# Lightning attention with an MLP on one core: q and k of tiles from the tenth on transposed by the DMA crossbar, head pairs on the row halves of TensorE

## The chip, the core and the metric

The kernel runs on one core of a Trainium2 chip. Work is done by four compute engines, each with its own in-order instruction stream: TensorE (PE in the profile, with its weight loads listed as PEld), VectorE (DVE), ScalarE (ACT) and GpSimd (POOL). SyncE (SP) only issues transfers. PE writes its results to PSUM, a small accumulation memory; DVE and ACT read PSUM, POOL doesn't. The metric is the device time of one execution in microseconds (us); lower is better.

## The reference

Two layers follow each other. The first is linear attention with a decay `lam` for each head, on q, k, v of shape 4 x 8 x 768 x 64 (batch, heads, positions, head size), in blocks, with a running state `kv_state`:

```python
intra = np.einsum('bhic,bhjc->bhij', qb, kb) * Dmask[None]      # lam**(i-j), i >= j
intra = np.einsum('bhij,bhjd->bhid', intra, vb)
inter = np.einsum('bhid,bhde->bhie', qb * lam_pow[None], kv_state)
out[:, :, sl] = intra + inter
kv_state = lam_block * kv_state + np.einsum('bhsd,bhse->bhde', kb * rev_pow, vb)
```

The second takes x (4 x 768 x 512, the heads side by side), normalises each row and adds an MLP: `x + relu(((x - mu) / std * g_ln) @ w_ch1) @ w_ch2`, with `w_ch1` of 512 x 2048 and `w_ch2` of 2048 x 512.

## The kernel before

**Tiles.** The 3072 rows are cut into NT = 24 tiles of 128 positions, six for each batch element (`nb` = 6), so a state starts anew at tiles 0, 6, 12 and 18. Tiles are counted from 0 here: the tenth is tile 9. NP = 4 is the number of head pairs; a pair fills 128 columns.

**Attention of one tile t.** It is split into steps that are called by name:

- `load_tile` (L56): three transfers of 256 KB for k, q and v, issued on SP; `after_pool` puts a POOL memset ahead so that the load starts no earlier than POOL's stream gets there.
- `p0` (L293): issues the loads of tile t+4 (with two exceptions), then on POOL casts k to bf16 (`kb`) and scales q and v by powers of lam (`qb`, `vb`).
- `p1` (L149): PE transposes `kb` and `qb`, four 128x128 blocks each, into PSUM (`tk`, `tq`). ACT copies `tk` in two halves into `kTp`, a buffer whose other halves stay zero, so that each head of a pair has a 128-row operand of its own. `tq` is copied to `qT`, by ACT in the first four tiles and by DVE later.
- `p2` (L170): the next state (`pk` on PE, sum on DVE, product with `lamC` on POOL into `Sn`), then the scores: eight matmuls `sc` (L192), one for each head, over 128 rows of which 64 are zero, and two DVE products with the mask `tril` into `mA`.
- `p3` (L198): PE forms `po` (eight matmuls with `mA`, four with the state); ACT copies it to `x`; DVE computes mean and variance of `x` (L212, L214) and the centred, scaled `xc` (L216).
- `p4` (L219): `xc` is transposed into the group's `xT`, by PE and ACT for tiles under 8, by a DMA transpose on SP from tile 8 on; then 1/std.

**MLP.** Tiles go through it in groups (`sizes`, L288). `m1` (L250) multiplies 16 blocks of 128 columns of w1 with the group's `xT` (N = 128 times the tiles of the group; groups of one or two tiles take four or two blocks in a unit) and ACT applies relu into `hT`. `m2` (L266) multiplies `hT` with w2, four matmuls of N = 512 in a unit, four units for each tile; the last ends in the DVE operation `o` (L282) and in a store on SP (L284).

**Order.** Every engine executes in the order in which the code issues. The start is written out by hand (L319 to L342), with the weight loads `load_w1` and `load_w2` (1 MB each, read in float32 and written as bf16, issued by POOL). Then come the units of groups 0 to 3 with a table `after` that puts attention steps between them, and from L373 on a planner: `plan` is the list of MLP units of the groups from 4 on, `steps` the list of attention steps in rounds (`round_of`, L306), and after each unit as many steps are issued as `pace` asks for, so that each group's last `p4` is issued some seven units ahead of its first unit. SP's stream is shared by loads, stores and DMA transposes.

Of the kernel before, what the change touches and what calls it, by code (L numbers as in the profile page):

```python
# [7 lines left out]
F32 = mybir.dt.float32  # L8
BF16 = mybir.dt.bfloat16
# [7 lines left out]
def kernel(  # L17
# [38 lines left out]
    def load_tile(t, after_pool=False):  # L56
        b, c = divmod(t, nb)
        got = {}
        for name, src in (("k", k), ("q", q), ("v", v)):
            f = inp.tile([128, H, D], F32, tag=name + "in", name=name + "in")  # L60
            if after_pool:

                nc.gpsimd.memset(f[:, 0, 0:1], 0.0)
                after_pool = False
            nc.sync.dma_start(f, src[b, :, c * C:(c + 1) * C, :].rearrange("h p d -> p h d"))  # L65
            got[name] = f
        qkv_in[t] = got
# [65 lines left out]
    mv_keep = {}  # L133
    xT_of = {}

    def in_k(t, eng):
        kb = wk.tile([128, H, D], BF16, tag="kb", bufs=4, name="kb")
        (eng.copy if eng is nc.scalar else eng.tensor_copy)(kb, qkv_in[t]["k"])  # L138
        st[t] = dict(kb=kb)

    def in_qv(t):
        f = qkv_in.pop(t)
        qb = wk.tile([128, H, D], BF16, tag="qb", name="qb")
        nc.gpsimd.tensor_tensor(qb, f["q"], lam_q[:, :, None].to_broadcast([128, H, D]), op=ALU.mult)  # L144
        vb = wk.tile([128, H, D], BF16, tag="vb", bufs=4, name="vb")
        nc.gpsimd.tensor_tensor(vb, f["v"], lam_v[:, :, None].to_broadcast([128, H, D]), op=ALU.mult)  # L146
        st[t].update(qb=qb, vb=vb)

    def p1(t):  # L149
        s = st[t]  # L150
        tk = ps.tile([128, NP, 128], BF16, tag="aux", bufs=2, name="tk")
        for p in range(NP):
            nc.tensor.transpose(tk[:, p, :], s["kb"][:, 2 * p:2 * p + 2, :], ident)  # L153
        kT = kTp[t % 2]
        nc.scalar.copy(kT[0:64, :, 0, :], tk[0:64, :, :])  # L155
        nc.scalar.copy(kT[64:128, :, 1, :], tk[64:128, :, :])  # L156
        if t < 4:
            tq = ps.tile([128, NP, 128], BF16, tag="mm", bufs=3, name="tq")
        else:
            tq = ps.tile([128, NP, 128], BF16, tag="aux", bufs=2, name="tq")  # L160
        for p in range(NP):
            nc.tensor.transpose(tq[:, p, :], s["qb"][:, 2 * p:2 * p + 2, :], ident)  # L162
        qT = wk.tile([128, NP, 128], BF16, tag="qT", name="qT")
        if t < 4:
            nc.scalar.copy(qT, tq)
        else:
            nc.vector.tensor_copy(qT, tq)  # L167
        s["kT"], s["qT"] = kT, qT

    def p2(t):  # L170
        s = st[t]
        c = t % nb
        s["S"] = state.get("S") if c > 0 else None
        if c < nb - 1:
            pk = ps.tile([128, NP, 128], F32, tag="aux", bufs=2, name="pk")
            for p in range(NP):
                nc.tensor.matmul(pk[:, p, :], lhsT=s["kb"][:, 2 * p:2 * p + 2, :], rhs=s["vb"][:, 2 * p:2 * p + 2, :],  # L177
                                 start=(p == 0), stop=(p == NP - 1), skip_group_check=True)
            Sn = wk.tile([128, NP, 128], BF16, tag="S", name="Sn")
            if c == 0:  # L180
                nc.vector.tensor_tensor(Sn, pk, lamC, op=ALU.mult)
            else:
                tmp = wk.tile([128, NP, 128], F32, tag="Stmp", bufs=2, name="Stmp")
                nc.vector.tensor_tensor(tmp, pk, state["S"], op=ALU.add)  # L184
                nc.gpsimd.tensor_tensor(Sn, tmp, lamC, op=ALU.mult)  # L185
            state["S"] = Sn
        mA = wk.tile([128, H, 128], BF16, tag="mA", name="mA")
        for half in range(2):
            sc = ps.tile([128, H // 2, 128], F32, tag="sc", bufs=2, name="sc")
            for i in range(H // 2):  # L190
                h = half * (H // 2) + i
                nc.tensor.matmul(sc[:, i, :], lhsT=s["kT"][:, h // 2, h % 2, :], rhs=s["qT"][:, h // 2, :],  # L192
                                 start=(i == 0), stop=(i == H // 2 - 1), skip_group_check=True)
            nc.vector.tensor_tensor(mA[:, half * (H // 2):(half + 1) * (H // 2), :], sc,  # L194
                                    tril[:, None, :].to_broadcast([128, H // 2, 128]), op=ALU.mult)
        s["mA"] = mA

    def p3(t):  # L198
        s = st[t]
        po = ps.tile([128, H, D], F32, tag="po", bufs=1, name="po")  # L200
        inter = s["S"] is not None
        for h in range(H):
            nc.tensor.matmul(po[:, h, :], lhsT=s["mA"][:, h, :], rhs=s["vb"][:, h, :],  # L203
                             start=(h == 0), stop=(not inter and h == H - 1), skip_group_check=True)
        if inter:
            for p in range(NP):
# [9 lines left out]
        nc.vector.scalar_tensor_tensor(xc, in0=x, scalar=mv[:, 0:1], in1=g_row, op0=ALU.subtract, op1=ALU.mult)  # L216
        s["xc"], s["mv"], s["x"] = xc, mv, x

    def p4(t):  # L219
# [65 lines left out]

        return m1, m2

    sizes = [2, 2, 1, 1, 2, 2, 3, 4, 4, 3]  # L288
    groups = [list(range(sum(sizes[:i]), sum(sizes[:i + 1]))) for i in range(len(sizes))]
    assert groups[-1][-1] == NT - 1  # L290
    group_of = {t: g for g, ts in enumerate(groups) for t in ts}

    def p0(t):  # L293
        for n in {4: (), 5: (8, 9)}.get(t, (t + 4,)):
            if n < NT:
                load_tile(n)
        in_k(t, nc.gpsimd)
        in_qv(t)


    def p3_p0(t):
# [2 lines left out]
            p0(t + 3)  # L304

    def round_of(j):  # L306
        steps = [(p1, j), (p3_p0, j - 1), (p2, j)]
        if j <= 11:
            steps.append((p4, j - 1))
        elif j > 12:  # L310
            steps.append((p4, j - 2))
        return [(f, t) for f, t in steps if t < NT]

    def run(*steps):
        for f, *a in steps:
            f(*a)


    for t in range(2):  # L319
        in_k(t, nc.vector)  # L320
        in_qv(t)
# [9 lines left out]
    in_qv(3)  # L331
    load_w1(1)
    load_tile(4, after_pool=True)
    run((p2, 2), (p4, 0), (p1, 3), (p3, 2))
    load_w1(2)
    load_w1(3)
    run((p2, 3), (p4, 1), (p0, 4))
    for c in range(NWC):
        load_w2(c)
    load_tile(5, after_pool=True)  # L340
# [30 lines left out]


    steps = []  # L373
    for j in range(8, NT + 2):
        steps += [s for s in round_of(j) if s not in ((p3_p0, 7), (p4, 7))]

    def upto(g):
# [48 lines left out]
```

## Time and profile before

| | us |
|---|---|
| median of 3 runs (236.11 to 236.44) | 236.11 |
| the profiled execution | 235.61 |
| its span, first to last instruction | 233.9 |
| PE busy (1792 matmuls) | 212.4 |
| ACT / DVE / POOL busy | 114.3 / 113.3 / 90.1 |

The profile has rows for each group of instructions by source line (L...), the chain of work that ended last, and, for chosen stretches, the busy time of each engine. A `pm` is a product of `m1` (L258) or `m2` (L271); `kin`, `qin`, `vin` are the loaded inputs, `w` a weight. The operations of before that the change touches on ACT and DVE:

```profile
L155 ACT COPY kTp<-tk 64x512 bf16<-64x512 bf16 x24 | 13.7, 572 | 31.4 <-PE tk L153 31.4
...
L216 DVE SCALAR_TENSOR_TENSOR xc<-x,mv,g_row 128x512 bf16<-128x512 f32 x24 | 20.7, 862 | 0.9
...
L167 DVE COPY qT<-tq 128x512 bf16<-128x512 bf16 x20 | 8.4, 419 | 15.2 <-PE tq L162 15.1
...
L156 ACT COPY kTp<-tk 64x512 bf16<-64x512 bf16 x24 | 13.9, 581 | 0.6
```

Read: line, engine, operation, output and input, shape and type, count; then busy us and mean ns of one; then the engine's idle time just before them and what ended it.

### The profile page before, as it was taken

The page shows a single profiled execution, that of the slowest core. Times are in us where ns is not written, and L with a number is a line of the kernel's source. Part 1 is how long each engine was busy: PE and PEld are TensorE (multiplying, and loading weights), DVE is VectorE, ACT ScalarE, POOL GpSimd, SP SyncE. Part 2 cuts the span into 40 slices and gives each one's busy share as a digit, 9 for nine tenths or more (in the row PEclk, how much of TensorE's full clock was granted, in tenths as well). Part 3 has the DMA queues.
Part 4 walks back from the last instruction along what each step waited for, and adds up shares of the span by engine and source line. Part 5 has one row for each costly group of instructions (what it writes and reads, how often), then busy time and mean ns, then how long its engine had stood idle before and what let it go on. Part 6 is the DMA issues. An engine that isn't in the chain of part 4 may idle for free.

```text
span 233.9 us, 4503 instructions
## 1 busy us (share of the span) xinstructions
PE 212.4 (91%) x1792; PEld 136.8 (58%) x1792; DVE 113.3 (48%) x219; ACT 114.3 (49%) x222; POOL 90.1 (39%) x103
## 2 busy tenths in 40 slices
PE   0664899999999899989999999999999999999992
PEld 0453879644977596579567655555554544456540
DVE  3459530334665567868776656653573223220021
ACT  5765486421546465367437832678213664017400
POOL 2659526216834667952746940633220000000000
PEclk9997799999999999999999999999999999999998
DMA  6998996999999999999999903310011200411012
GB/s 125 221 225 113 221 176 89 182 217 205 225 209 300 204 242 227 209 210 243 168 249 229 160 3 112 93 22 3 34 66 59 67 0 3 125 60 39 3 66 70
DMA packets 91717, 32.02 MB, mean 137 GB/s; under 512 B 84272, under 2 KB 88624, under 8 KB 91696
## 3 DMA queue, kind: packets, MB, share of 16 engines
q1 hardware_dynamic: 87328, 27.53, 58.7%
q0 software_dynamic: 4224, 4.19, 11.3%
q8 instruction: 14, 0.23, 0.4%
q14 instruction: 7, 0.06, 0.1%
q10 hardware_dynamic: 144, 0.00, 0.0%
HBM read 27.53 MB, written 6.29 MB: 145 GB/s over the span
## 4 chain that ended last, share of the span: by engine, by line
PE 70%; DMA 15%; SPq 4%; POOL 4%; DVE 3%; ACT 2%; issue 1%; DVEq 0%; ACTq 0%
PE pm L271 30%; PE pm L258 28%; DMA vin<-in_v_dram 7%; DMA w<-in_moe_w_ch_dram 6%; SPq L65 4%; PE sc L192 3%; PE po L203 2%; DMA xT<-xc 2%; PE tq L162 2%; PE po L207 1%; PE tk L153 1%; POOL vb L146 1%; PE pk L177 1%; DVE xc L216 1%; POOL w L78 1%
## 5 line engine op out<-in xcount | busy, mean ns | idle before, releaser
L258 PE MATMUL pm<-xT,w 128*128 128x256 bf16 (+3 forms) x640 | 90.4, 294 | 1.5 <-DMA xT<-xc 0.8
L271 PE MATMUL pm<-w,hT 128*128 128x512 bf16 x384 | 88.6, 379 | 0.1
L261 ACT ACTIVATE hT<-pm 128x512 bf16<-128x512 f32 (+1 forms) x104 | 58.2, 565 | 44.5 <-PE pm L258 43.6
L258 PEld LDWEIGHTS <-w 128*128 128x128 bf16 x640 | 56.2, 98 | 25.4 <-DMA xT<-xc 1.0
L271 PEld LDWEIGHTS <-hT 128*128 128x128 bf16 x384 | 36.3, 98 | 38.0 <-issue 0.4
L185 POOL TENSOR_TENSOR Sn<-Stmp,lamC 128x512 bf16<-128x512 f32 x16 | 20.4, 1273 | 60.9 <-DVE Stmp L184 60.9
L212 DVE BATCH_NORM_STATS2 stats<-x 128x6 f32<-128x512 f32 x24 | 16.7, 694 | 43.6 <-ACT x L210 43.5
L282 DVE SCALAR_TENSOR_TENSOR o<-pm,rstd,x 128x512 f32<-128x512 f32 (+1 forms) x25 | 18.0, 725 | 33.6 <-PE pm L271 33.3
L194 DVE TENSOR_TENSOR mA<-sc,tril 128x512 bf16<-128x512 f32 x48 | 30.7, 681 | 1.3 <-PE sc L192 1.3
L144 POOL TENSOR_TENSOR qb<-qin,lam_q 128x512 bf16<-128x512 f32 x24 | 25.6, 1066 | 13.7 <-DMA qin<-in_q_dram 13.6
L155 ACT COPY kTp<-tk 64x512 bf16<-64x512 bf16 x24 | 13.7, 572 | 31.4 <-PE tk L153 31.4
L146 POOL TENSOR_TENSOR vb<-vin,lam_v 128x512 bf16<-128x512 f32 x24 | 25.5, 1062 | 3.9 <-DMA vin<-in_v_dram 2.8
L210 ACT COPY x<-po 128x512 f32<-128x512 f32 x24 | 14.0, 585 | 16.0 <-PE po L207 12.5
L216 DVE SCALAR_TENSOR_TENSOR xc<-x,mv,g_row 128x512 bf16<-128x512 f32 x24 | 20.7, 862 | 0.9
L192 PE MATMUL sc<-qT,kTp 128*128 128x128 bf16 x192 | 16.4, 234 | 0.3 <-ACT kTp L156 0.2
L167 DVE COPY qT<-tq 128x512 bf16<-128x512 bf16 x20 | 8.4, 419 | 15.2 <-PE tq L162 15.1
L153 PE MATMUL tk<-ident,kb 128*128 128x128 bf16 x96 | 10.0, 231 | 6.1 <-DVE kb L138 5.5
L138 POOL CAST kb<-kin 128x512 bf16<-128x512 f32 x20 | 13.2, 661 | 5.7 <-DMA kin<-in_k_dram 5.5
L192 PEld LDWEIGHTS <-kTp 128*128 128x128 bf16 x192 | 13.5, 106 | 1.6 <-ACT kTp L156 0.4
L156 ACT COPY kTp<-tk 64x512 bf16<-64x512 bf16 x24 | 13.9, 581 | 0.6
L162 PE MATMUL tq<-ident,qb 128*128 128x128 bf16 x96 | 9.7, 227 | 3.9 <-POOL qb L144 3.5
L203 PEld LDWEIGHTS <-mA 128*128 128x128 bf16 x192 | 9.0, 99 | 6.7 <-DVE mA L194 3.4
(45 smaller groups left out, 112.5 us busy)
## 6 DMA issues: line engine op xcount, KB each, us to landing
kin<-in_k_dram SPq DMA_DIRECT2D x24, 256.0 KB, 4.9
qin<-in_q_dram SPq DMA_DIRECT2D x24, 256.0 KB, 5.0
vin<-in_v_dram SPq DMA_DIRECT2D x24, 256.0 KB, 5.4
out_dram<-o SPq DMA_DIRECT2D x23, 256.0 KB, 2.5
w<-in_moe_w_ch_dram POOLq DMA_DIRECT2D x8, 512.0 KB, 8.0
g_row<-in_moe_g_ln_dram SPq DMA_DIRECT2D x1, 256.0 KB, 5.0
xT<-xc SPq DMA_TRANSPOSE x16, 3.2
out_dram<-o SPq DMA_DIRECT2D x2, 128.0 KB, 1.7
```

The source lines that it names most:

```text
L144: nc.gpsimd.tensor_tensor(qb, f["q"], lam_q[:, :, None].to_broadcast([128, H, D]), op=ALU.mult)
L146: nc.gpsimd.tensor_tensor(vb, f["v"], lam_v[:, :, None].to_broadcast([128, H, D]), op=ALU.mult)
L162: nc.tensor.transpose(tq[:, p, :], s["qb"][:, 2 * p:2 * p + 2, :], ident)
L185: nc.gpsimd.tensor_tensor(Sn, tmp, lamC, op=ALU.mult)
L192: nc.tensor.matmul(sc[:, i, :], lhsT=s["kT"][:, h // 2, h % 2, :], rhs=s["qT"][:, h // 2, :], start=(i == 0), stop=(i == H // 2 - 1), skip ...
L194: nc.vector.tensor_tensor(mA[:, half * (H // 2):(half + 1) * (H // 2), :], sc, tril[:, None, :].to_broadcast([128, H // 2, 128]), op=ALU.mult)
L212: nc.vector.bn_stats(stats, x)
L216: nc.vector.scalar_tensor_tensor(xc, in0=x, scalar=mv[:, 0:1], in1=g_row, op0=ALU.subtract, op1=ALU.mult)
L258: nc.tensor.matmul(pm[:, b, :], lhsT=w1[n // W2K][:, kk, (n % W2K) * 128:(n % W2K + 1) * 128], rhs=xT_of[g][:, kk, 0:N], start=(b == 0 and ...
L261: nc.scalar.activation(hT[:, u * NB:(u + 1) * NB, 0:N], pm, ACT.Relu)
L271: nc.tensor.matmul(acc[i], lhsT=hT[:, kk, i * 128:(i + 1) * 128], rhs=w2[kk // W2K][:, kk % W2K, :], start=(kk == 0), stop=(kk == KB - 1))
L282: nc.vector.scalar_tensor_tensor(o[:, sl], in0=a[:, sl], scalar=rstd, in1=x[:, sl], op0=ALU.mult, op1=ALU.add)
```

## The change

1. From tile 9 on (`XB = 9`), `kb` and `qb` are the two halves of one tile `kq` (128 x 1024 bf16), and `p1` is one DMA transpose on SP of `kq` into `kqT`, in place of eight PE transposes and the copies. It stands one round earlier than `p1` did.
2. In all tiles the scores take the two heads of a pair from partitions 0 to 63 and 64 to 127 of `kT` and `qT`, with 64-row operands, and write to two PSUM tiles, one for each half; the zero-padded `kTp` and its memsets go, and in tiles 0 to 8 ACT copies `tk` once.
3. `xc` is computed from `po` in PSUM and no longer from `x`.
4. `p0` loads tile t+2 and no longer t+4. The groups are 2, 2, 1, 1, 2, 2, 2, 3, 3, 3, 3 tiles, so `m1` runs at N up to 384. `p4` of tile j-1 is in round j throughout.
5. At the start the scores stand ahead of the state; `load_w1(0)` is issued before `vb` of tile 2, the POOL product of a state after the inputs of the next tile, and the first `p4` steps are in other places.

The diff, cut to its core:

```diff
-    kTp = []
-    for i in range(2):
-        kt = const.tile([128, NP, 2, 128], BF16, name=f"kTp{i}")
-        nc.vector.memset(kt, 0.0)
-        kTp.append(kt)
+    XB = 9
+
     def in_k(t, eng):
-        kb = wk.tile([128, H, D], BF16, tag="kb", bufs=4, name="kb")
+        if t >= XB:
+            kq = wk.tile([128, 2, H, D], BF16, tag="kq", bufs=4, name="kq")
+            kb, qb = kq[:, 0], kq[:, 1]
...
     def p1(t):
         s = st[t]
+        if t >= XB:
+            kqT = wk.tile([128, 2 * NP, 128], BF16, tag="kqT", name="kqT")
+            nc.sync.dma_start_transpose(kqT, s["kq"].rearrange("p a h d -> p (a h d)"))
+            s["kT"], s["qT"] = kqT[:, 0:NP, :], kqT[:, NP:2 * NP, :]
+            return
...
-        kT = kTp[t % 2]
-        nc.scalar.copy(kT[0:64, :, 0, :], tk[0:64, :, :])
-        nc.scalar.copy(kT[64:128, :, 1, :], tk[64:128, :, :])
+        kT = wk.tile([128, NP, 128], BF16, tag="kT", name="kT")
+        nc.scalar.copy(kT, tk)
...
+    def scores(t):
+        s = st[t]
+        mA = wk.tile([128, 2, NP, 128], BF16, tag="mA", name="mA")
+        sc = [ps.tile([128, NP, 128], F32, tag="sc", bufs=2, name=f"sc{e}") for e in range(2)]
+        for p in range(NP):
+            for e in range(2):
+                half = slice(e * D, (e + 1) * D)
+                nc.tensor.matmul(sc[e][:, p, :], lhsT=s["kT"][half, p, :], rhs=s["qT"][half, p, :],
+                                 start=(p == 0), stop=(p == NP - 1), skip_group_check=True)
+        for e in range(2):
+            nc.vector.tensor_tensor(mA[:, e], sc[e], tril[:, None, :].to_broadcast([128, NP, 128]), op=ALU.mult)
...
-                nc.gpsimd.tensor_tensor(Sn, tmp, lamC, op=ALU.mult)
+                s["pool"] = lambda: nc.gpsimd.tensor_tensor(Sn, tmp, lamC, op=ALU.mult)
...
-        nc.vector.scalar_tensor_tensor(xc, in0=x, scalar=mv[:, 0:1], in1=g_row, op0=ALU.subtract, op1=ALU.mult)
+        nc.vector.scalar_tensor_tensor(xc, in0=po.rearrange("p h d -> p (h d)"), scalar=mv[:, 0:1], in1=g_row, op0=ALU.subtract, op1=ALU.mult)
...
-    sizes = [2, 2, 1, 1, 2, 2, 3, 4, 4, 3]
+    sizes = [2, 2, 1, 1, 2, 2, 2, 3, 3, 3, 3]
...
     def p0(t):
-        for n in {4: (), 5: (8, 9)}.get(t, (t + 4,)):
-            if n < NT:
-                load_tile(n)
+        if 5 < t < NT - 2:
+            load_tile(t + 2)
...
     def round_of(j):
-        steps = [(p1, j), (p3_p0, j - 1), (p2, j)]
-        if j <= 11:
-            steps.append((p4, j - 1))
-        elif j > 12:
-            steps.append((p4, j - 2))
+        steps = [(p1, j)] if j < XB else []
+        if j + 1 >= XB:
+            steps.append((p1, j + 1))
+        steps += [(p3_p0, j - 1), (p2, j)]
+        steps.append((p4, j - 1))
...
-    run((p1, 0), (p2, 0), (p1, 1), (p3, 0))
+    run((p1, 0), (scores, 0), (next_state, 0), (p1, 1), (scores, 1), (p3, 0), (next_state, 1))
     in_k(2, nc.scalar)
-    in_qv(2)
+    in_q(2)
     load_w1(0)
-    run((p2, 1), (p1, 2), (p3, 1))
+    in_v(2)
+    fin_state(1)
+    run((p1, 2), (scores, 2), (p3, 1), (next_state, 2))
...
-    run((p2, 2), (p4, 0), (p1, 3), (p3, 2))
+    run((p4, 0), (p1, 3), (scores, 3), (p4, 1), (p3, 2))
```

Three places show how the order moves. The first is PE's stream at tile 9, from the end of its state product `pk` into its scores; before, where `kTp_131` is the padded buffer of odd tiles:

```order
L177 LDWEIGHTS kb
L177 MATMUL pk<-vb,kb 128x128
L192 LDWEIGHTS kTp_131
L192 MATMUL sc<-qT,kTp_131 128x128
L192 LDWEIGHTS kTp_131
L192 MATMUL sc<-qT,kTp_131 128x128
```

and now, where `sc_1360` and `sc_1361` are the PSUM tiles of the even and the odd heads:

```order
L198 LDWEIGHTS kq
L198 MATMUL pk<-vb,kq 128x128
L185 LDWEIGHTS kqT
L185 MATMUL sc_1360<-kqT 128x128
L185 LDWEIGHTS kqT
L185 MATMUL sc_1361<-kqT 128x128
```

The count of score matmuls is the same, eight; they alternate between two outputs and take weights and moving operand from `kqT`, which a DMA writes. The eight transposes `tk` and `tq` of the tile (L153, L162) are gone from PE's stream.

The second place is SP's stream at the first DMA transposes of `xc`, those of tiles 8 and 9; before, with the loads of tile 16 between them and those of tile 17 behind:

```order
L227 DMA_TRANSPOSE xT<-xc 128x4x128
L65 DMA kin<-in_k_dram 128x8x64
L65 DMA qin<-in_q_dram 128x8x64
L65 DMA vin<-in_v_dram 128x8x64
L227 DMA_TRANSPOSE xT<-xc 128x4x128
L284 DMA out_dram<-o 128x512
```

and now, with `kqT` of tile 11 and the loads of tile 14 between the two, and `kqT` of tile 12 behind:

```order
L248 DMA_TRANSPOSE xT<-xc 128x4x128
L156 DMA_TRANSPOSE kqT<-kq 128x8x128
L65 DMA kin<-in_k_dram 128x8x64
L65 DMA qin<-in_q_dram 128x8x64
L65 DMA vin<-in_v_dram 128x8x64
L248 DMA_TRANSPOSE xT<-xc 128x4x128
L305 DMA out_dram<-o 128x512
L156 DMA_TRANSPOSE kqT<-kq 128x8x128
```

One DMA transpose of twice the size has come into each round, and the loads beside it are of a tile nearer at hand.

The third place is POOL's stream at the start, from the inputs of tile 2 to the last load of w1; before:

```order
L144 TENSOR_TENSOR qb<-qin,lam_q 128x512
L146 TENSOR_TENSOR vb<-vin,lam_v 128x512
L75 DMA w_0_75<-in_moe_w_ch_dram 128x4x512
L185 TENSOR_TENSOR Sn<-Stmp,lamC 128x512
L144 TENSOR_TENSOR qb<-qin,lam_q 128x512
L146 TENSOR_TENSOR vb<-vin,lam_v 128x512
L75 DMA w_1_76<-in_moe_w_ch_dram 128x4x512
L63 MEMSET kin 128x1
L185 TENSOR_TENSOR Sn<-Stmp,lamC 128x512
L75 DMA w_2_77<-in_moe_w_ch_dram 128x4x512
L75 DMA w_3_78<-in_moe_w_ch_dram 128x4x512
```

and now:

```order
L145 TENSOR_TENSOR qb<-qin,lam_q 128x512
L75 DMA w_0_75<-in_moe_w_ch_dram 128x4x512
L149 TENSOR_TENSOR vb<-vin,lam_v 128x512
L206 TENSOR_TENSOR Sn<-Stmp,lamC 128x512
L145 TENSOR_TENSOR qb<-qin,lam_q 128x512
L149 TENSOR_TENSOR vb<-vin,lam_v 128x512
L75 DMA w_1_76<-in_moe_w_ch_dram 128x4x512
L206 TENSOR_TENSOR Sn<-Stmp,lamC 128x512
L63 MEMSET kin 128x1
L75 DMA w_2_77<-in_moe_w_ch_dram 128x4x512
L75 DMA w_3_78<-in_moe_w_ch_dram 128x4x512
```

The first weight load has passed `vb` of tile 2, and the memset that lets the loads of tile 4 go on SP has fallen behind the state product of tile 2.

More of the change, by code (lines that the diff above doesn't have):

```diff
@@ L168, in p1, with next_state @@
         s["kT"], s["qT"] = kT, qT
-    def p2(t):
+    def scores(t):
[9 more added lines that the diff above has]
+            nc.vector.tensor_tensor(mA[:, e], sc[e], tril[:, None, :].to_broadcast([128, NP, 128]), op=ALU.mult)
+        s["mA"] = mA
+    def next_state(t):
         s = st[t]
@@ L184, in p2, with fin_state @@
                 nc.vector.tensor_tensor(tmp, pk, state["S"], op=ALU.add)
-                nc.gpsimd.tensor_tensor(Sn, tmp, lamC, op=ALU.mult)
+                s["pool"] = lambda: nc.gpsimd.tensor_tensor(Sn, tmp, lamC, op=ALU.mult)
             state["S"] = Sn
[L187 to L196, printed above, removed]
+    def fin_state(t):
+        f = st[t].pop("pool", None)
+        if f:
+            f()
+    def p2(t):
+        next_state(t)
+        fin_state(t)
+        scores(t)
     def p3(t):
@@ L202, in p3 @@
         for h in range(H):
-            nc.tensor.matmul(po[:, h, :], lhsT=s["mA"][:, h, :], rhs=s["vb"][:, h, :],
+            nc.tensor.matmul(po[:, h, :], lhsT=s["mA"][:, h % 2, h // 2, :], rhs=s["vb"][:, h, :],
                              start=(h == 0), stop=(not inter and h == H - 1), skip_group_check=True)
@@ L293, in p0 @@
     def p0(t):
-        for n in {4: (), 5: (8, 9)}.get(t, (t + 4,)):
-            if n < NT:
-                load_tile(n)
+        if 5 < t < NT - 2:
+            load_tile(t + 2)
         in_k(t, nc.gpsimd)
-        in_qv(t)
+        in_q(t)
+        in_v(t)
     def p3_p0(t):
@@ L320 @@
         in_k(t, nc.vector)
-        in_qv(t)
+        in_q(t)
+        in_v(t)
     lam_cp = lam_c.rearrange("p (a two) -> p a two", two=2)
@@ L373 @@
     steps = []
-    for j in range(8, NT + 2):
+    for j in range(8, NT + 1):
         steps += [s for s in round_of(j) if s not in ((p3_p0, 7), (p4, 7))]
```

23 lines of the change are left out of this document (14 added, 9 removed).

## The prediction

> **What bounds the kernel now.** I read the chain that ended last first, in order of time (start, us, what).
>
> ```profile
> 23.55 11.34 DMA vin<-in_v_dram
> 34.96 1.04 POOL vb L146
> 36.01 2.22 POOL w L78 x3
> 38.22 13.75 DMA w<-in_moe_w_ch_dram
> 52.02 4.48 PE pm L271 x20
> 56.49 0.22 PE tk L153 x4
> 56.72 0.22 PE tq L162 x4
> 56.94 1.73 PE pm L271 x8
> 58.66 0.45 PE sc L192 x8
> ```
>
> Up to 52.02 the chain is made of transfers: v of tile 4, the POOL product that waits for it, and behind that product in POOL's stream the issue of w2, whose last quarter lands at 51.97. From there on it is PE. The busy time of PE in stretches (stretch, length, PE busy, matmuls, clock, DMA share, GB/s) says how full PE is:
>
> ```profile
> 52.02:229.56 177.54, 174.71 (x1452) 1.00 0.63 128
> 66.00:106.00 40.00, 37.20 (x429) 1.00 1.12 231
> 106.00:229.56 123.56, 123.52 (x882) 1.00 0.41 84
> ```
>
> All of PE's 2.83 us of idle time after 52 lies between 66 and 106. PE's timeline has it in five places (start, length, instruction, [idle before, releaser]):
>
> ```profile
> 70.88 0.38 PE L234 MATMUL xt<-ident,xc 128*128 128x128 bf16 x4 [0.47 <-DVE qT L167]
> 77.61 0.40 PE L234 MATMUL xt<-ident,xc 128*128 128x128 bf16 x4 [0.85 <-DVE xc L216]
> 81.57 0.56 PE L192 MATMUL sc<-qT,kTp 128*128 128x128 bf16 x7 [0.22 <-ACT kTp L156]
> 100.12 1.05 PE L258 MATMUL pm<-xT,w 128*128 128x256 bf16 x8 [0.85 <-DMA xT<-xc]
> 104.67 0.38 PE L162 MATMUL tq<-ident,qb 128*128 128x128 bf16 x4 [0.40 <-DVE Sn L181]
> ```
>
> So there are two stages: until 52 the time is that of DMA, and work taken from PE there is worth nothing; after 52 each us taken from PE's stream is a us of the result, as long as no new wait opens.
>
> **The change part by part**, against the profiled execution (235.61, span 233.9; the median of the runs is 0.5 above it).
>
> *Transposes of tiles 9 to 23.* Four `tk` and four `tq` cost PE 0.22 + 0.22 in the chain above, at every tile. Fifteen tiles: 15 x 0.44 = **6.6 us less**, all after 52. The trace shows these transposes back to back at 55 ns each. The Trainium skill (TensorE: Matmul & The Clock Gate, Part 4) gives some 275 ns for a transpose in a kernel's context; by it the 120 would be worth 33 us, an estimate from that page; the row of this trace decides.
>
> *Scores on row halves.* Tiles 5 to 23 run their scores after 52: 19 times 0.45, 56 ns a matmul. If the two halves run side by side, eight matmuls take the time of four, 0.22, and 19 x 0.23 = 4.4 us go. Against that stands what PE loses when it changes between full and half operands, twice for each tile. No row of before has half operands. The nearest rows bound it: differently shaped neighbours (transposes, N = 64, N = 512) follow each other without a gap, so nothing; or the whole length of one score matmul less its step.
>
> ```profile
> L192 PE MATMUL sc<-qT,kTp x192: 219/219/314, 9.2 to 187.4; 128*128 128x128 bf16 x192
> ```
>
> That is 219 - 56 = 163 ns a change, 0.33 a tile. The tile then takes 0.22 to 0.55 in place of 0.45: from -4.4 to +1.9 us over 19 tiles. I take half the price, since neither end has a row of its own kind: 0.39, **1.1 us less**. If the halves don't overlap at all, the price stands without the gain: +6.3.
>
> The Trainium skill has both sides (TensorEngine Tiling (Array Packing), Theoretical Speedup and Key Properties): two row tiles give up to twice the speed, and a change of the tiling mode drains TensorE. No run here shows either yet; the page gives no length of a drain.
>
> *MLP groups.* The steps of `m1` by N are in the chain:
>
> ```profile
> 105.05 0.87 PE pm L258 x8
> ...
> 122.77 1.30 PE pm L258 x8
> ...
> 150.88 1.73 PE pm L258 x8
> ```
>
> That is 0.109 at N = 256, 0.163 at 384, 0.216 at 512. Before: 256, 128 and 128 of them, 76.4 us; now 320 and 256, none at 512, 76.6; the 128 of single-tile groups stay. Some **0.1 us more**.
>
> *The start.* The single copy of `tk`, the missing memsets and the earlier scores shorten the way to the first `m1`, at 26.50 before, though `xc` of tile 1 was ready at 21.5 (one row each from the timelines of DVE, POOL and PE):
>
> ```profile
> 18.90 2.63 DVE L216 SCALAR_TENSOR_TENSOR xc<-x,mv,g_row 128x512 bf16<-128x512 f32 x1
> 22.22 1.26 POOL L185 TENSOR_TENSOR Sn<-Stmp,lamC 128x512 bf16<-128x512 f32 x1 [0.39 <-DVE Stmp L184]
> 26.50 2.10 PE L258 MATMUL pm<-xT,w 128*128 128x256 bf16 x16 [0.67 <-ACT xT L235]
> ```
>
> The transposes (0.40) and their copy (0.59) must still come between, so up to 3 to 4 us could be won there. It is covered: w2 lands at 51.97 whatever PE does, because its issue waits for v of tile 4. On POOL that load's memset has fallen behind a 1.26 us product, so the three loads leave SP up to 1.3 later. But w1 keeps the DMA engines at work meanwhile and the bytes are the same. **Nothing**, bounds -0.4 (w1's last quarters leave earlier by the 0.39 wait) to +1.3. If the cover goes, the start is worth -3.
>
> *Copies and centring.* ACT loses 48 half copies for 9 whole ones, DVE 15 copies `qT`. Both engines are half idle and no chain after 52 but two of the waits runs through them. `xc`, 862 ns on average in the row shown with the profile of before, is with a PSUM input like `o`, the same kind of operation:
>
> ```profile
> L282 DVE SCALAR_TENSOR_TENSOR o<-pm,rstd,x 128x512 f32<-128x512 f32 (+1 forms) x25 | 18.0, 725 | 33.6 <-PE pm L271 33.3
> ```
>
> No slower, so nothing; `po` is held some 2 us longer, and the next `p3` is a round away.
>
> *Waits.* The 0.22 goes (the second copy of `tk`), the 0.40 too (no `tq` left that needs a PSUM buffer): **0.6 us less**. The 0.47 and 0.85 at `xt` stay, since tiles 6 and 7 still go po, copy, mean, `xc`, transpose, with one or two units between. What is new is that PE's score weights of tile 9 on wait for a DMA, with PE's whole stream behind them. And SP, in order, holds loads, `kqT`, `xT` and stores: a `kqT` that waits for POOL's `qb` holds back the next loads, and an `xT` waits behind them. SP's price of each (start, us):
>
> ```profile
> 62.61 1.13 SPq L65 DMA_DIRECT2D qin<-in_q_dram  x1
> ...
> 93.86 0.52 SPq L65 DMA_DIRECT2D kin<-in_k_dram  x1
> 94.48 0.53 SPq L65 DMA_DIRECT2D qin<-in_q_dram  x1
> 95.10 0.87 SPq L65 DMA_DIRECT2D vin<-in_v_dram  x1
> 96.06 1.55 SPq L227 DMA_TRANSPOSE xT<-xc  x1
> 97.71 0.53 SPq L284 DMA_DIRECT2D out_dram<-o  x1
> ```
>
> and of all DMA transposes (min/median/max, ns on SP, then us from issue to landing):
>
> ```profile
> L227 SPq DMA_TRANSPOSE xT<-xc x16: 1191/1518/1924, 92.3 to 203.1; - x16
> ...
> DMA to landing us min/median/max: 2.4/3.2/5.9
> ```
>
> `kqT` is two of these: 2.4 to 3.8 on SP, some 3 in the middle, and a landing 1 to 2 later than that of an `xT`, 4 to 8. A round then costs SP 1.9 for loads, 1.5, 3.0 and 0.5, together **7.0**. A round of PE, from the first transposes of tile 8 to the last `po`:
>
> ```profile
> 79.59 0.39 PE L153 MATMUL tk<-ident,kb 128*128 128x128 bf16 x4
> 195.19 0.40 PE L203 MATMUL po<-vb,mA 128*128 128x64 bf16 x8
> ```
>
> is 115.6 / 16 = 7.2, less about 0.5 now, 6.7. SP is just at PE's pace, and falls behind by 0.3 a round over the 13 rounds that still load, 4 us. `kqT` is issued about one and a half rounds ahead of its scores, 10 us, and outlasts that. `xT` has about six us from its issue to the group's first unit, so one or two group starts may wait as the one at 100.12 does, by 0.85. I leave that one as it is, and put the new waits at 0, bounds 0 and +4.
>
> Sum: 235.6 - 6.6 - 1.1 + 0.1 + 0 - 0.6 = 227.4 for a profiled execution, **227.9** for the median.
>
> **The rivals.**
>
> - *The halves run for nothing.* No cost of a change, as for all other changes of shape in the trace: 3.3 us more go, 224.6. For it: eight `po` weight loads pass in 0.23 us, so weights can follow at the 28 ns that this needs. Against: no row with half operands.
> - *The price of a change is the full 0.163.* Two a tile cost more than the overlap gives: 3.0 more than the forecast, 230.9. It is the drain rule named above, with a length from the row of L192.
> - *The halves don't do what is said*: the two matmuls of a pair run one after the other and pay the changes too, 227.9 + 6.3 + 1.1 = 235.3, no measurable or a small gain.
> - *The start counts after all*: w2 lands earlier with PE, 3 us less, 224.9. Against: its issue stands behind the load of tile 4 in both orders.
> - *SP becomes the bound, slower than before.* If loads cost 1.13 each, as at 62.61, SP's round is 3.4 + 1.55 + 3.1 + 0.5 = 8.6. Over 13 rounds its lag grows by 1.9 each, 25 us, of which 10 are the lead of `kqT`: 15 us of waits, 227.9 + 15 = 243. It decides from a round of SP above 6.7 + 10/13 = 7.5, and makes the kernel slower than before from 8.1. For it: loads cost that much wherever DMA was full. Against: they did so when loads ran four tiles ahead; now they go at PE's pace, and at 93 to 98 with transposes between them they took 0.5 to 0.9.
>
> **How the numbers follow.** Forecast 0.38, free halves 0.27, full price of the change 0.18, halves without effect 0.05, the start 0.05, SP as the bound 0.07. The likeliest gives 227.9. The range takes in free halves with some more waits gone (223.5) and the full price with a us of new waits (232): it leaves out the halves without effect and SP as the bound, 0.12, and some tails. A measurement here can tell about 0.2% (0.5 us) from no change. Faster: all but two cases, 0.88. Slower: SP, 0.07. Same: the rest, 0.05.
>
> **What would show it.** Before 52, the last w2 still lands near 52 and PE waits for it longer than the 0.25 or so of before. After 52, PE's stream has no `tk` and `tq` from tile 9 on, and the chain has eight score matmuls in 0.39; 0.22 or 0.55 and more tell the rivals. PE's idle time between 66 and 106 is about 2.2. SP's DMA transposes of `kqT` take 2.4 to 3.8 and land before their scores; a wait `sc <- DMA kqT`, tile after tile, shows the slow case. I'm wrong if PE is idle after 106, or if w2 lands more than a us away from 52.

## The result and the profile after

The changed kernel took **227.72 us** (median of 4 runs, 227.62 to 228.95) against 236.11 (236.04 to 236.44) before: a ratio of **0.965**, 95% interval 0.962 to 0.969. Its profiled execution took 227.68, with a span of 226.0. One execution of e2 below (232.26) fell into a slower state of the core and is left out of its median and range.

The stretches of PE that were shown of before (stretch, length, PE busy, matmuls, clock, DMA share, GB/s) now read:

```profile
53.05:221.85 168.80, 167.65 (x1397) 1.00 0.77 157
66.00:106.00 40.00, 38.89 (x424) 1.00 1.16 218
106.00:221.85 115.85, 115.81 (x838) 1.00 0.60 128
```

53.05 is the begin of the fourth round of `m2`, the first work that needs the last quarter of w2; it stood at 52.02. From there PE needs 168.8 where it needed 177.5. PE's timeline has the waits that matter:

```profile
29.29 0.40 PE L255 MATMUL xt<-ident,xc 128*128 128x128 bf16 x4 [0.54 <-DVE xc L237]
31.27 10.57 PE L279 MATMUL pm<-xT,w 128*128 128x256 bf16 x80 [1.59 <-DMA w<-in_moe_w_ch_dram]
...
71.66 0.40 PE L255 MATMUL xt<-ident,xc 128*128 128x128 bf16 x4 [0.24 <-DVE xc L237]
78.30 0.40 PE L255 MATMUL xt<-ident,xc 128*128 128x128 bf16 x4 [0.75 <-DVE xc L237]
```

After 53, two of before's five waits are left. Ahead of it stands something new: the 80 matmuls at 31.27 take 10.57 us (before, the same 80 took 8.90), since the granted clock was 0.64 from 31.27 to 36.00. The chain shows a tile's steps (start, us, what):

```profile
130.51 0.65 PE pm L279 x4
131.16 0.22 PE pk L198 x4
131.38 0.33 PE sc L185 x8
131.72 4.66 PE pm L279 x28
```

No `tk`, no `tq`; the eight scores take 0.33 in place of 0.45 (the experiments show that another 0.10 stands ahead of them). The view of the source line of the new DMA transposes:

```profile
L156 SPq DMA_TRANSPOSE kqT<-kq x15: 1242/1283/2167, 81.5 to 175.6; - x15
...
DMA to landing us min/median/max: 3.0/3.2/4.6
```

In the median they cost SP 1.28 and land in 3.2, about what an `xT` of half the size takes (1.23 and 3.5 here).

### The profile page after: what moved, and what is told of

Read it like the earlier page. It is cut to its first block, busy times and chain, and to the rows that moved or that the text cites. A ratio compares the mean times of both kernels' runs of the same rounds, so it can differ in the third digit from the quotient of the medians.

```text
span 226.0 us, 4339 instructions
## 1 busy us (share of the span) xinstructions
PE 206.9 (92%) x1736; PEld 131.4 (58%) x1736; DVE 104.5 (46%) x202; ACT 95.5 (42%) x191; POOL 88.0 (39%) x103
## 4 chain that ended last, share of the span: by engine, by line
PE 81%; DMA 6%; DVE 4%; SPq 3%; ACT 2%; issue 1%; POOL 1%; DVEq 0%
PE pm L292 36%; PE pm L279 35%; DMA w<-in_moe_w_ch_dram 4%; PE sc L185 3%; SPq L65 3%; DMA qin<-in_q_dram 2%; PE po L224 2%; PE po L228 2%; PE pk L198 1%; DVE stats L233 1%; ACT x L231 1%; DVE xc L237 1%; PE tq L169 1%; DVE Stmp L205 1%; PE xt L255 1%
## 5 line engine op out<-in xcount | busy, mean ns | idle before, releaser
L279 PE MATMUL pm<-xT,w 128*128 128x256 bf16 (+2 forms) x704 | 92.2, 287 | 1.6 <-DMA w<-in_moe_w_ch_dram 1.6
L282 ACT ACTIVATE hT<-pm 128x384 bf16<-128x384 f32 (+1 forms) x112 | 60.0, 536 | 57.9 <-PE pm L279 57.2
L279 PEld LDWEIGHTS <-w 128*128 128x128 bf16 x704 | 63.6, 100 | 23.9 <-DMA w<-in_moe_w_ch_dram 1.8
L292 PEld LDWEIGHTS <-hT 128*128 128x128 bf16 x384 | 36.2, 98 | 39.2
L237 DVE SCALAR_TENSOR_TENSOR xc<-po,mv,g_row 128x512 bf16<-128x512 f32 x24 | 18.0, 751 | 2.3
L145 POOL TENSOR_TENSOR kq<-qin,lam_q 128x512 bf16<-128x512 f32 x15 | 15.7, 1044 | 1.2 <-DMA qin<-in_q_dram 1.2
L145 POOL TENSOR_TENSOR qb<-qin,lam_q 128x512 bf16<-128x512 f32 x9 | 9.4, 1042 | 15.3 <-DMA qin<-in_q_dram 14.7
L205 DVE TENSOR_TENSOR Stmp<-pk,Sn 128x512 f32<-128x512 f32 x16 | 10.9, 683 | 4.2 <-PE pk L198 4.1
L224 PE MATMUL po<-vb,mA 128*128 128x64 bf16 x192 | 10.4, 199 | 0.1
L141 POOL CAST kq<-kin 128x512 bf16<-128x512 f32 x15 | 9.2, 611 | 2.0 <-DMA kin<-in_k_dram 2.0
L258 ACT ACTIVATE std<-mv,eps_t 128x1 f32<-128x1 f32 x24 | 7.0, 293 | 5.4 <-DVE mv L235 5.4
```

The costliest lines, as they stand in the source:

```text
L145: nc.gpsimd.tensor_tensor(st[t]["qb"], qkv_in[t]["q"], lam_q[:, :, None].to_broadcast([128, H, D]), op=ALU.mult)
L224: nc.tensor.matmul(po[:, h, :], lhsT=s["mA"][:, h % 2, h // 2, :], rhs=s["vb"][:, h, :], start=(h == 0), stop=(not inter and h == H - 1), ...
L237: nc.vector.scalar_tensor_tensor(xc, in0=po.rearrange("p h d -> p (h d)"), scalar=mv[:, 0:1], in1=g_row, op0=ALU.subtract, op1=ALU.mult)
L279: nc.tensor.matmul(pm[:, b, :], lhsT=w1[n // W2K][:, kk, (n % W2K) * 128:(n % W2K + 1) * 128], rhs=xT_of[g][:, kk, 0:N], start=(b == 0 and ...
L282: nc.scalar.activation(hT[:, u * NB:(u + 1) * NB, 0:N], pm, ACT.Relu)
L292: nc.tensor.matmul(acc[i], lhsT=hT[:, kk, i * 128:(i + 1) * 128], rhs=w2[kk // W2K][:, kk % W2K, :], start=(kk == 0), stop=(kk == KB - 1))
```

## The experiments

All are edits of the changed kernel. They ran on other chips, on which the kernel before took 236.5 to 237.1 with a wider spread, so each has its ratio to the runs beside it. The last four columns are of the profiled execution: where the fourth round of `m2` begins; from there to PE's last matmul; PE's waits of 0.15 and more in that stretch; and the difference of the two, PE's **work**.

| kernel | median us (range) | ratio, 95% | round 4 | to the end | waits | work |
|---|---|---|---|---|---|---|
| before | 236.11 | 1 | 52.02 | 177.50 | 2.79 | 174.71 |
| after | 227.72 (227.62-228.95) | 0.962-0.969 | 53.05 | 168.76 | 0.99 | 167.77 |
| e2 halves apart | 228.68 (228.27-229.44) | 0.959-0.971 | 52.55 | 171.04 | 2.89 | 168.15 |
| e3 `pk` between | 230.40 (230.09-230.68) | 0.967-0.977 | 52.74 | 171.94 | 1.00 | 170.94 |
| f1 one half | 232.01 (231.17-233.78) | 0.972-0.986 | 55.22 | 172.71 | 1.00 | 171.71 |
| e4 PE transposes | 235.09 (233.76-236.62) | 0.989-0.998 | 53.83 | 175.11 | 1.00 | 174.11 |
| f2 full rows | 234.49 (234.02-235.14) | 0.983-0.995 | 51.84 | 176.13 | 1.44 | 174.69 |
| g2 loads far | 237.93 (235.40-238.93) | 1.002-1.009 | 52.78 | 179.08 | 8.72 | 170.36 |
| g3 centre x | 228.49 (228.09-228.94) | 0.963-0.968 | 53.03 | 170.15 | 2.40 | 167.75 |
| e1 load 4 first | 228.29 (227.73-228.62) | 0.958-0.968 | 52.86 | 169.91 | 1.83 | 168.08 |
| f3 w2 early | 229.88 (227.95-230.35) | 0.961-0.974 | 52.68 | 171.43 | 3.74 | 167.69 |
| f4 w1, w2 early | 228.00 (227.77-228.13) | 0.955-0.967 | 51.52 | 170.74 | 3.04 | 167.70 |
| g1 tile 4 early | 227.37 (226.67-228.41) | 0.958-0.967 | 51.64 | 169.20 | 1.25 | 167.95 |
| h1 start | 227.28 (226.66-227.88) | 0.958-0.964 | 51.90 | 170.06 | 2.37 | 167.69 |

Work repeats within 0.4 us between kernels that issue the same PE instructions at the full clock (g2's fell, see there), so it separates what PE does from what it waits for.

### What the scores on row halves are worth

**e2** takes the halves one after the other.

```diff
-        for p in range(NP):
-            for e in range(2):
+        for e in range(2):
+            for p in range(NP):
```

> The eight score matmuls of a tile issued as four of the even heads and then four of the odd ones, nothing else changed. In the changed kernel a tile's scores take 0.42 us from the end of the matmul ahead to the start of the one behind, against 0.45 before. Theory A, the halves of a pair overlap (0.22) and the rest is two changes of the operand height at 0.10 each: apart, the matmuls take 0.45 + 0.20 = 0.65 a tile, and 19 tiles make the kernel 4.4 us longer, 232.1. Theory B, the halves don't overlap, and a 64-row matmul is simply shorter: no change, 227.7 within 0.3.

**e3** puts `pk` between the second and the third pair (`scores(t, next_state)` for `next_state(t)` and `scores(t)`; the diff is cut to its core).

```diff
+            if p == 1 and between:
+                between(t)
```

> The state product pk of a tile (four full-height matmuls) is put between the second and third pair of its scores, so each tile with a state product has four changes of operand height and not two; the matmuls are the same. Theory A, a change costs 0.10 us: 15 tiles after 53 us with two more changes, 3.0 us longer, 230.7. Theory B, a change costs nothing and the 0.42 of the scores is incomplete overlap: within 0.3 of 227.7.

**f1** uses one half alone: it leaves out the odd heads' scores and computes those of the even heads twice.

```diff
-                half = slice(e * D, (e + 1) * D)
+                half = slice(0, D)
```

> The odd heads' scores are left out: the even heads' operands are used twice, so that all eight score matmuls of a tile lie on the same row half. Theory A (the two halves of a pair run side by side on PE, each half no faster than a full matmul): with one half there is nothing beside it, eight score matmuls take 0.44 in place of 0.22, +0.22 a tile, x19 = +4.2 us: about 232. Theory B (a matmul of 64 rows by itself comes every 28 ns, whichever half it is on): nothing changes, 227.7, and the eight still take 0.22.

The rows of one tile in PE's timelines, first of the changed kernel, then of e2, e3 and f1. Read the starts; the lengths count each matmul's way through the array, so that neighbours overlap:

```profile
130.35 0.81 PE L279 MATMUL pm<-xT,w 128*128 128x384 bf16 x4
131.00 0.39 PE L198 MATMUL pk<-vb,kq 128*128 128x128 bf16 x4
131.32 0.40 PE L185 MATMUL sc<-kqT 64*128 64x128 bf16 x8
131.65 4.72 PE L279 MATMUL pm<-xT,w 128*128 128x384 bf16 x28
```

```profile
132.69 0.39 PE L198 MATMUL pk<-vb,kq 128*128 128x128 bf16 x4
133.01 0.41 PE L185 MATMUL sc<-kqT 64*128 64x128 bf16 x8
133.35 3.91 PE L279 MATMUL pm<-xT,w 128*128 128x384 bf16 x23
```

```profile
131.95 0.81 PE L280 MATMUL pm<-xT,w 128*128 128x384 bf16 x4
132.70 0.29 PE L185 MATMUL sc<-kqT 64*128 64x128 bf16 x4
132.91 0.40 PE L200 MATMUL pk<-vb,kq 128*128 128x128 bf16 x4
133.24 0.29 PE L185 MATMUL sc<-kqT 64*128 64x128 bf16 x4
133.46 3.75 PE L280 MATMUL pm<-xT,w 128*128 128x384 bf16 x22
```

```profile
135.36 0.39 PE L198 MATMUL pk<-vb,kq 128*128 128x128 bf16 x4
135.68 0.62 PE L185 MATMUL sc<-kqT 64*128 64x128 bf16 x8
136.23 0.99 PE L279 MATMUL pm<-xT,w 128*128 128x384 bf16 x5
```

In the changed kernel the four `pm` (0.163 each) end their steps at 131.00 and `pk` follows without a gap. Four `pk` are 0.22, so 0.10 lies between `pk` and `sc`; of the 0.33 from `sc` to the next `pm` another 0.11 lies behind the scores. In e3 the same twelve matmuls have four changes of height in place of two, and take 0.86 (from 131.95 + 0.65 = 132.60 to 133.46) in place of 0.65: **0.10 a change**. Its work is 3.17 more; 15 of the tiles from 5 on have a `pk`, and 15 x 0.21 = 3.2.

f1 decides between overlap and a short step: on one half alone the eight take 0.55 in place of 0.33, 0.22 more a tile, and the work is 3.94 more, 0.21 for each of the 19 tiles. So **the two halves do run side by side**: eight in 0.22, or 28 ns each, against 55 without a partner. The single records of the trace say the same: in the changed kernel's tile above, the scores start in pairs, 3 or 4 ns apart within a pair and some 55 from one pair's start to the next (67 from the first); in f1 they start one by one, as far apart as these pairs. e2's time came out as its theory B forecast, no change, but f1 excludes B's reason. In e2 the scores start in pairs as well, 13 or 14 ns apart. So the pairs need not be neighbours in the stream: even heads first and odd heads behind them cost 0.01 a tile, where one half after the other would cost 0.22.

### Transposes on PE, and the scores on full rows beside them

**e4** leaves all transposes of q and k on PE.

```diff
-    XB = 9
+    XB = 24
```

> The changed kernel with the DMA transposes of q and k undone (XB = 24): tiles 9 to 23 are transposed on PE again, with one copy of k on ACT and one of q on DVE. Theory A, each tile's transposes were 0.446 us of PE's stream and nothing else: 15 x 0.446 = 6.7 us longer, 234.4. Theory B, the DMA transposes also gave waits or queueing on SP that go with them: less than 6.2 longer. Theory C, the copies on ACT and DVE had delayed PE as well: more than 7.2 longer.

**f2** is e4 with before's padded `kTp`: two half copies on ACT, and scores on all 128 rows (the line of the scores alone is shown).

```diff
-                nc.tensor.matmul(sc[e][:, p, :], lhsT=s["kT"][half, p, :], rhs=s["qT"][half, p, :],
+                nc.tensor.matmul(sc[e][:, p, :], lhsT=s["kT"][:, p, e, :], rhs=s["qT"][:, p, :],
```

> To be read against the kernel with all transposes on PE (e4, 235.1; its span 233.3, of which 178.5 lie after the fourth round of m2 begins): here the scores too are as before the change, padded kT on all 128 rows. Theory A (a change of operand height costs 0.10, two a tile, and eight half matmuls save 0.22): the scores of a tile go from 0.42 to 0.45, x19 = +0.5 us after 54; the two more copies of a tile on ACT may open a wait of 0.2 or so as in the kernel before. Theory B (the price of a change is the whole 0.163): the full rows are faster, 19 x -0.10 = -1.9. Theory C (changes are free): +3.3 to +4.4.

e4's work is 6.34 more than after's, **0.42 a tile**. Its profiled execution is 7.3 longer, which alone would look like theory C, but 0.8 of that is a later round 4 and 0.2 lies behind PE's last matmul; the work is near theory A's 6.7. f2's is 0.58 more than e4's, 0.03 a tile: that is all that the halves bring, net of the two changes. And f2's 174.69 is before's 174.71: with these two undone nothing of the work is left to explain, so the new group sizes are worth nothing measurable there. Two of f2's waits (PE's timeline) are before's as well:

```profile
70.70 0.38 PE L260 MATMUL xt<-ident,xc 128*128 128x128 bf16 x4 [0.47 <-ACT kTp L169]
...
81.29 0.56 PE L190 MATMUL sc<-qT,kTp 128*128 128x128 bf16 x7 [0.22 <-ACT kTp L169]
```

So the second copy of `tk` was worth 0.22 + 0.22 of waits (e4 has 0.25 where f2 has 0.47). Neither e4 nor f2 has before's 0.40 at `tq` or its 0.85 for `xT`, though both keep all `tq` on PE.

### How far loads run ahead

**g2** brings back only the loads four tiles ahead.

```diff
-        if 5 < t < NT - 2:
-            load_tile(t + 2)
+        for n in {4: (), 5: (8, 9)}.get(t, (t + 4,)):
+            if n < NT:
+                load_tile(n)
```

> Loads run four tiles ahead as before the change, all else as after. Theory A (the waits for xT went because loads no longer stand in front of the transposes on SP): PE waits again for an xT or a kqT at 85 to 105, by 0.8 to 3 us together, 228.5 to 231. Theory B (they went because PE's stream begins a us later and the rest is chance): no more than 0.3 of new waits, 227.7.

It gives the whole gain back. SP's timeline, and PE's:

```profile
81.89 0.38 SPq L65 DMA_DIRECT2D kin<-in_k_dram  x1
82.36 0.83 SPq L65 DMA_DIRECT2D qin<-in_q_dram  x1
83.28 1.40 SPq L65 DMA_DIRECT2D vin<-in_v_dram  x1
84.77 0.95 SPq L65 DMA_DIRECT2D kin<-in_k_dram  x1
85.81 1.21 SPq L65 DMA_DIRECT2D qin<-in_q_dram  x1
87.15 1.05 SPq L65 DMA_DIRECT2D vin<-in_v_dram  x1
88.31 1.08 SPq L305 DMA_DIRECT2D out_dram<-o  x1
89.88 2.76 SPq L156 DMA_TRANSPOSE kqT<-kq  x2
```

```profile
85.95 0.39 PE L198 MATMUL pk<-vb,kq 128*128 128x128 bf16 x4
94.07 0.61 PE L185 MATMUL sc<-kqT 64*128 64x128 bf16 x8 [7.73 <-DMA kqT<-kq]
94.61 3.60 PE L279 MATMUL pm<-xT,w 128*128 128x256 bf16 x16
```

The input of tile 9's transpose was ready as early as in the changed kernel (POOL's product for it starts at 75.50 here, 75.76 there). But two more tiles' loads stand ahead of it on SP, 6.3 us at about 1 us a load, and behind them one more store; it leaves at 89.88 in place of 81.50. PE waits **7.73**, and then runs at a granted clock of 0.50 from 94 to 98 and 0.75 from 98 to 102, which accounts for the 2.6 of work: 10.3 together. Afterwards the loads of k and q mostly cost some 0.6 each between transposes, those of v about 1.0 and more, and no further tile waits. More was lost than theory A's 0.8 to 3.

### Centring from the SBUF copy

**g3**: `in0=x` for `in0=po...` in `xc`.

> Centring reads the SBUF copy x again. Theory A (the source is worth nothing: xc takes 0.75 to 0.86 either way, and DVE is half idle): 227.7 within 0.5, the waits at xt of tiles 6 and 7 grow by 0.1 or so each. Theory B (reading PSUM is what shortened the waits at xt and xT): they go back to 0.47 and 0.85 and a wait for xT of 0.5 or more appears; 228.5 to 229.

The work is the same; the waits at `xt` change by -0.06 and +0.11, and waits of 0.34 for `kqT` and 1.02 for `xT` appear. That looks like theory B, but the first `kqT` leaves SP at 83.04 in this execution, and both waits stand as well in e2 and f3, which do centre from PSUM and whose first `kqT` leaves at 82.78 and 83.22. The range of the times, 228.09 to 228.94, lies within the changed kernel's. What the edit is worth, if anything up to some 0.8, stays open.

### The start

**e1**: tile 4's loads let go ahead of the state product of tile 2.

```diff
-    fin_state(2)
     load_tile(4, after_pool=True)
+    fin_state(2)
```

> The changed kernel with one step of the start put back: POOL's memset and the loads of tile 4 stand ahead of the state product of tile 2 again. In the changed kernel the fourth m2 round (the first unit that needs the last quarter of w2) starts at 53.05 us, 1.0 later than before, though m1 began 2.9 earlier. Theory A, the loads of tile 4 left SP 0.9 later and so w2 was issued at 36.9 and not 35.95: the last w2 lands at 52 again and the kernel is 0.9 to 1.0 us shorter, 226.7. Theory B, PE waited for w1 at 31.27 and ran the next 4.7 us at a granted clock of 0.64, which costs it 1.8: the unit stays at 53.0 and the time within 0.3 of 227.7, with w2 landing earlier but unused.

**f3**: half of w2 issued ahead of tile 4's products.

```diff
-    run((next_state, 3), (fin_state, 3), (p0, 4))
-    for c in range(NWC):
+    run((next_state, 3), (fin_state, 3))
+    for c in range(2):
+        load_w2(c)
+    p0(4)
+    for c in range(2, NWC):
         load_w2(c)
```

> The first two loads of w2 are issued on POOL ahead of tile 4's products, at about 28 in place of 37, so that they fill the stretch from 34 to 38 in which DMA is idle. Theory A (the begin of the fourth round of m2, at 53, is set by the landing of w2): w2 lands 3 us earlier, the round begins at 50 to 51, 225 to 226. Theory B (PE's own stream sets it, through its wait for w1 at 30 and the slow clock behind it): w2 lands earlier and no wait for it is left, but m1 and the first rounds of m2 take as long as before, and the round begins at 52.5 to 53; 227.5. w1 and tile 4 could land later by the shared DMA: then up to +1.

**f4**: also `load_w1(2)` ahead of `fin_state(2)`.

> The same, and the third quarter of w1 is issued ahead of the state product of tile 2, 1.25 us earlier. Theory A and B of the run before join here: if both w2 and the wait for w1 with its slow clock hold PE, only this kernel gains both. B: the wait for w1 at 30 shrinks from 1.6 to some 0.3, the clock stays at 1.00, 80 matmuls take 8.9 in place of 10.6, and the fourth round begins at about 50.5: 225.3. If w1 doesn't land earlier because DMA is full, the same as the run before.

The issue of w2 on POOL, first in the changed kernel, then in e1:

```profile
36.90 3.04 POOL L78 DMA_DIRECT2D w<-in_moe_w_ch_dram  x4
...
35.97 3.04 POOL L78 DMA_DIRECT2D w<-in_moe_w_ch_dram  x4
```

e1 moves it from 36.90 to 35.97, and PE hardly gains: it waits 1.42 for w1 at 31.09, and its 80 matmuls take 10.57 again. That is theory B; the time, 228.29, has 0.8 of waits for `xT` in it. Kernels with the same start whose clock stayed full (e2, e3, g2, g3) wait for w2 instead, by 0.4 to 0.5, and begin the round at 52.6 to 53.0. So w2 and PE's slow stretch end within half a us of each other at 53; shortening one shows the other. f3 delays w1 and the second half of w2 (issued at 43.74, as v of tile 4 came later), and its round begins 0.4 earlier. Its time, 229.88, fits neither theory: PE then waits 1.68 for the first `kqT` and 1.07 for an `xT`. f4 takes away both: no wait for w1, clock 1.00, the round at 51.52. But its time hardly moved. Its PE timeline shows where 1.5 us went:

```profile
30.04 8.90 PE L279 MATMUL pm<-xT,w 128*128 128x256 bf16 x80
...
85.63 0.40 PE L185 MATMUL sc<-kqT 64*128 64x128 bf16 x8 [0.56 <-DMA kqT<-kq]
98.29 3.69 PE L279 MATMUL pm<-xT,w 128*128 128x256 bf16 x32 [1.49 <-DMA xT<-xc]
```

The first `kqT` left SP at 81.42, as in the changed kernel (81.50), while PE came 1.5 earlier. In the changed kernel it lands 86.1 at the latest (81.50 + 4.6, the longest landing), and PE reads it at 86.53: the changed kernel has at least 0.4 us between PE and **a second bound, the chain of loads and transposes on SP**. The two last kernels try to move both.

**g1**: tile 4's loads behind `in_q(3)`, `load_w1(2)` ahead of `fin_state(2)`.

> Tile 4's three loads are let go about 19.6 in place of 22.8, behind the q product of tile 3 on POOL, and the third quarter of w1 is issued ahead of the state product of tile 2. DMA's two gaps (21 to 24 and 34 to 38) should close: v of tile 4 lands near 30, w2 is issued from about 31, 6 us earlier, and the loads of tiles 5 to 7 behind it too. Theory A (right behind PE lies the chain of loads and DMA transposes from 54 to 100; the start is worth what both of them gain): PE does not wait for w1 or w2, the fourth round of m2 begins at 50.5 to 51.5, the waits for kqT and xT at 86 to 100 that took back the 1.5 us of the run before are at most 0.5, and the time is 225.0 to 226.0. Theory B (loads from tile 8 on are held to PE's pace by the stores ahead of them on SP, so that the chain does not move with the start): the fourth round begins as early, but 1 to 2 us come back as waits for kqT or xT, 227.0 to 227.7.

**h1**: f4's w1; tile 4's loads ahead of `fin_state(2)`; and w2 between the products:

```diff
-    run((next_state, 3), (fin_state, 3), (p0, 4))
+    run((next_state, 3), (fin_state, 3))
+    in_k(4, nc.gpsimd)
+    in_q(4)
     for c in range(NWC):
         load_w2(c)
+    in_v(4)
```

> The candidate: the third quarter of w1 is issued ahead of tile 4's loads, those ahead of the state product of tile 2, and w2 between the q and the v product of tile 4, so that its issue waits for q alone. Theory A (PE and the chain of loads and transposes behind it both move): PE has no wait for w1 or w2, the fourth round of m2 begins at 50 to 51, kqT of tile 9 leaves SP a us or more earlier than in the changed kernel (81.5), the waits for kqT and xT stay under 0.5: 225.0 to 226.0. Theory B (from 54 to 100 the transfers set the pace and don't move, as the run with w1 and w2 earlier looked): 1.5 to 2.5 of the gain come back as waits for kqT and xT at 85 to 100, 227 to 227.7.

g1's trace comes nearest to theory A: round 4 at 51.64, the first `kqT` at 80.34, one wait of 0.25 for `xT`, work and waits as after. But w1 now lands later, and PE waits for it twice, where A had no such wait:

```profile
28.20 1.92 PE L279 MATMUL pm<-xT,w 128*128 128x256 bf16 x16 [1.55 <-DMA w<-in_moe_w_ch_dram]
...
31.53 8.91 PE L279 MATMUL pm<-xT,w 128*128 128x256 bf16 x80 [1.19 <-DMA w<-in_moe_w_ch_dram]
```

And its median, 227.37, lies in theory B's range (the profiled execution took 226.71). h1 has round 4 at 51.90, bounded by w2 again, and its first `kqT` at 81.58:

```profile
51.90 4.48 PE L292 MATMUL pm<-w,hT 128*128 128x512 bf16 x20 [0.45 <-DMA w<-in_moe_w_ch_dram]
...
85.72 0.40 PE L185 MATMUL sc<-kqT 64*128 64x128 bf16 x8 [0.27 <-DMA kqT<-kq]
97.98 3.69 PE L279 MATMUL pm<-xT,w 128*128 128x256 bf16 x32 [1.10 <-DMA xT<-xc]
```

It is theory B's picture. Both medians, 227.37 and 227.28, are below the changed kernel's and their ratios (0.962 and 0.961) too, but the intervals overlap with its 0.962 to 0.969, and f4 has 0.961 with a median above it: a gain over it of up to half a per cent is possible, not shown. Over the kernel before both are clearly faster.

## Why the prediction was right

227.9 was forecast, 227.4 for a profiled execution; they were 227.7 and 227.68. The mechanism of the main terms held. That the number is so close is in part luck: the start cost 1.0 more than forecast and transposes, scores and groups together gave 0.7 less, while the waits gave 1.2 more and the end 0.2.

- *Transposes*, forecast -6.6: measured **-6.3** (e4). The 33 us that the prediction worked out from the Trainium skill's 275 ns a transpose (TensorE: Matmul & The Clock Gate, Part 4) are excluded.
- *Scores*, forecast -1.1 at half the price of a change: **-0.6** (f2 against e4). The halves overlap as assumed, eight in 0.22 (f1). The term that was mis-sized is the change of height, 0.10 (e3) where 0.082 was taken; two of them turn 0.39 a tile into 0.42. Free halves, the full price and halves without effect all fall. The Trainium skill (TensorEngine Tiling (Array Packing), Key Properties) says that a change of mode drains TensorE. These runs show 0.10 us at each change, which agrees with that; that PE drains in this time, no trace here shows.
- *MLP groups*, +0.1: nothing to be seen in the work of f2, 174.69 against before's 174.71.
- *The start*, forecast 0 with bounds -0.4 and +1.3: **+1.0**, inside the bounds. The step named was the right one, tile 4's loads behind the 1.26 us product: they left SP at 22.79 in place of 21.86, and w2's issue came 0.95 later. That was put at nothing because the bytes are the same, which was wrong: DMA was half idle then (a share of 0.61 from 21 to 24, where full stretches have 1.2) and again later (0.05 from 34.5 to 36.9). The last quarter of w2, issued at 39.2, landed at 53.0. And PE alone was no earlier, which the prediction lacked: `m1` began 2.9 earlier, ran into w1 (1.59), and then had the slow clock, 0.64 over 4.7 us.
- *Waits*, forecast -0.6: **-1.8**. The 0.22 went as forecast, and half of the 0.47 with it (f2); the 0.40 went too, but need not have gone because `tq` left PE (e4 keeps `tq` and lacks the wait). The 0.85 for `xT`, which I left, went in this execution; in g1, e1, g3, e2, f3, h1 and f4 0.2 to 1.5 of such a wait is back. Which edits removed these two waits isn't settled: the new group sizes and the place of `p4` were not tried by themselves.
- *SP*: the price of `kqT` was forecast as that of two `xT`, 3.0, and its landing as 4 to 8; measured 1.28 and 3.0 to 4.6. So SP's round, by the forecast's own sum, is 1.9 + 1.2 + 1.3 + 0.5 = 4.9 rather than 7.0, and it doesn't fall behind in the steady state. But the rival "SP as the bound" was nearer than its 0.07 and its form was wrong: not a lag that grows with each round, but a single one at the first transposes, while DMA is full. g2 shows it with the loads as they were: 237.9, half a per cent slower than before (ratio 1.002 to 1.009). The shorter reach of the loads is thus the part of the change on which the gain stands, and I had not priced it.
- The end: PE's last matmul to the end of the execution went from 6.1 to 5.9, -0.2.

Sum: +1.0 - 6.3 - 0.6 - 1.8 - 0.2 = -7.9; 235.61 to 227.68 is -7.93.

Of the signs named beforehand: w2 was to land within a us of 52 and did so barely, at 53.0; PE was to wait for it longer than the 0.25 of before and did not, its round begins without a wait of 0.15 or more; the scores with their two changes were to take 0.39 and take 0.42; PE idle between 66 and 106 was to be 2.2 and was 1.1; `kqT` on SP was to be 2.4 to 3.8 and was 1.3; after 106 PE is not idle.

## What to carry to other kernels

Work that was moved from PE to DMA transposes was won here only because their issue keeps clear of the loads in the same in-order queue (g2): look at what stands ahead of the first one, not at the mean of a round. Matmuls with 64 rows overlap in pairs on both halves, but every change of height costs about as much as two full 128-column matmuls: eight save 0.22 and two changes take 0.20 of it back, so gather more of them between two changes and keep full-height work from between. And where two bounds lie within half a us, as w2 and PE at 53 or PE and SP at 86, taking away one shows the other: split the time at the hand-over into begin, waits and work before judging an edit.

## What the hardware did that was not expected

- A DMA transpose of 128 x 1024 elements costs SP 1.28 us and lands in 3.2, one of 128 x 512 1.23 and 3.5 (medians of the changed kernel): between these two sizes neither grows.
- The halves overlap even if all matmuls of one half are issued ahead of all of the other (e2, 0.34 against 0.33).
- The slow clock doesn't follow the length of the wait. The 80 `m1` matmuls took 10.57 behind waits for w1 of 1.59, 1.42 and 1.54 (after, e1, e4), but 8.91 behind 2.69 and 2.67 (f1, f3). g2's 7.73 was followed by a clock of 0.50 for 4 us. The Trainium skill (TensorE: Matmul & The Clock Gate, Part 1) says that the gate looks at free-running windows of about 3.4 us and slows the clock after at least one idle one. g2's row agrees with that; the waits of 1.4 to 1.6 are shorter than a window, and why the clock fell behind them stays open. No run here tells where the windows lie.
